# Softcap attention with soft mixture-of-experts slots on one core: weight requests spaced by bytes, the third group's queries requested at the start, engine order recomputed

## The chip, the cores and the metric

The kernel runs on one core of a Trainium2 chip. The metric is the time of one execution on the device, in microseconds (us). The profile is of one execution; its engines are PE (matrix products), ACT (activation functions), DVE (elementwise work), POOL (elementwise work, and the requests of one kind of DMA) and SP (the requests of the other kind).

## The reference

Attention over 8 batches, 12 heads, 448 tokens and 64 features, with a tanh cap on the scores, then a soft mixture of experts with 8 experts of 4 slots each over the 3584 x 768 result:

```python
scores = cap * np.tanh(q @ k.T / sqrt(64) / cap)            # cap = 30, per batch and head
attn = exp(scores - max) / sum                              # softmax over the keys
x = (attn @ v) -> (3584, 768)
logits = x @ phi                                            # phi: (768, 32)
d = softmax(logits, over tokens); slot_input = d.T @ x      # 32 slots
slot_out[e] = relu(slot_input[e] @ w1[e]) @ w2[e]           # w1: (8, 768, 1024), w2: (8, 1024, 768)
out = softmax(logits, over slots) @ slot_out                # (3584, 768) float32
```

## The kernel before

**The work.** Attention runs over 24 groups Q = 0..23; a group is four heads of one batch, so three groups make a batch. The scores of a group are 14 tiles of 128 keys x 448 queries, taken in six chunks of 3, 2, 2, 2, 3 and 2 tiles. For each group:

- `SC` (PE, L515 and L518) makes a chunk of scores in one of two PSUM areas; `TH` (ACT, L528) applies tanh to it and so frees the area. Chunks 0 to 3 (nine tiles) go to the tile `exa`, chunks 4 and 5 (five tiles) to `exd`.
- `EX` (ACT, L536) takes the exponential of the nine tiles of `exa` in one instruction. The five tiles of `exd` are done on DVE instead: four `PH` steps (L543), each making one term of an approximation. There are two `term` buffers, so the third term waits until PE has read the first.
- `PV` (PE, L553) multiplies with the values: parts a0, a1 and d read `exa`, parts c0 to c3 read the four terms. `NR` (DVE, L586 and L587) divides by the sums and writes `xq`.
- `TX` and `CX` (PE L598, DVE L602) transpose `xq`; at the end of a batch `LG` (PE, L622) makes the logits, `EE` (ACT, L632) their exponential, and `ER`, `ET`, `CE`, `SS`, `CS` add the batch to the slot sums.

**The loads.** Queries of a group are requested by POOL (`L q`, L402, cast to bf16 under way, two buffers `qb`) and transposed on PE (`T q`, L485, tile `qps`), then copied by DVE (`C q`, L494). Keys (`LK`, L407, two buffers `kraw`) and values (`LV`, L417, two buffers `vraw`) are requested by SP as float32; `KC` (DVE, L411) casts the keys, and `VC` (POOL, L422) and `VS` (DVE, L425) cast and scale the values. A buffer's next request waits for the work that read it: the queries of group Q wait for `T q` of group Q - 2.

**The weights.** Beside attention POOL requests 56 weight parts (`W`): first 24 parts of w1 of 512 KB each (`w1b`, L338), then 27 parts of w2 of 384 KB that are cast into DRAM (`w2d`, L342) and 5 that stay on chip (`w2b`). These too are cast under way. After attention SP reads the 27 parts back (`w2t`, L867).

**The order.** Every engine works through its own list in order. The lists come from a planner, the class `Plan`: each step gets a due time from its place in the group plus a number of the table `DUE`, a time it may be held for from `HOLD`, and a cost from `COST`; `order()` places steps greedily on a model of the engines. Nothing of this runs on the chip: only the order is left. `load("q", 1)` is emitted ahead of the list. A weight part's due time on POOL is

```python
for k in range(self.parts):
    t = 3000 + k * (NQ * T - T) / self.parts
    op(("W", k), "POOL", C["issue"], (), t, after=t)
```

that is, the 56 parts at equal distances. On the chip a `W` waits for nothing but its turn in POOL's list.

**After attention** come the last group's logits, the slot sums, the first layer (`hp`, L888), the second (`so_ps`, L921) and the output products (L959, L1009), whose results SP stores.

Of the kernel before, what the change touches and what calls it, by code (L numbers as in the profile page):

```python
# [14 lines left out]
ACT = mybir.ActivationFunctionType  # L15
# [10 lines left out]
W = DH + 1  # L26
# [20 lines left out]
TERMS = ((-2.18104, 1.0), (-1.928978, 1.0), (-1.674805, 0.6953125), (-1.419015, 0.6953125))  # L47
PH = len(TERMS)

DUE = {"C0k": 81, "C0q": -150665, "CAk": -64995, "CAq": 68196, "CE": 14263, "CS": 66229, "CW": -188046, "CX":  # L50
# [7 lines left out]
HOLD = {"C0k": 463, "C0q": 1272, "CAk": 739, "CAq": 1395, "CE": 1500, "CW": 856, "Ck": 66, "ER": 1352, "ET": 416,  # L58
# [4 lines left out]
COST = dict(quad=9000, lat=200, dma=7000, form=90, sc=100, scm=200, act=0.833, act0=70, ts=0.265, ts0=70,  # L63
            pvf=31, turn=460, kturn=420, xturn=450, copy=610, norm=830, vcast=1060, vscale=340, kcast=650, kdiag=300,
            issue=800, load=1400, part1=2740, part2=2530, same=300, page=6000)


class Plan:
# [11 lines left out]
    def build(self):  # L80
        C, NQ, NQB = COST, self.NQ, self.NQB
        T = float(C["quad"])
        op = self.op
# [22 lines left out]
        for Q in range(NQ):  # L106
            b, t0, lastq = Q // NQB, Q * T, Q == NQ - 1
            for s in range(nc):
                t = t0 + first[s] * T / NQT
                prev = divmod(Q * nc + s - len(BANKS), nc)  # L110
                tiles = range(first[s], first[s] + CHUNKS[s])
                deps = [("TH",) + prev]
                if Q:
                    deps += [("C", "k", Q), ("C", "q", Q)]
                elif any(TILES[x][0] for x in tiles):
                    deps += [("C0", "k"), ("C0", "q")]
                m = sum(TILES[x][1] is None for x in tiles)
# [24 lines left out]
            te = t0 + .8 * T  # L142
            vs = [("VC", Q), ("VS", Q)]
            op(("PV", Q, "a0"), "PE", 24 * C["pvf"], [("EX", Q, 0)] + vs, te, take=True, mm=24)
            op(("PV", Q, "a1"), "PE", 8 * C["pvf"], [("PV", Q, "a0")], te + 1, mm=8)
            op(("NR", Q, 0), "DVE", C["norm"], [("PV", Q, "a1"), ("SS", (Q - 4) // NQB, 1)], te + 1000,
               give=("PV", Q, "a0"))
            td = t0 + T + 1200
            op(("PV", Q, "d"), "PE", (8 + 4 * (NA - 8)) * C["pvf"], [("EX", Q, 0)] + vs, td - 10, take=True, mm=8 + 4 * (NA - 8))
            for i in range(PH):  # L150
                op(("PV", Q, f"c{i}"), "PE", 4 * nd * C["pvf"],
                   [("PH", Q, i), ("PV", Q, f"c{i - 1}" if i else "d")], td + 1100 * i, mm=4 * nd)
            if ne:
                op(("PV", Q, "e"), "PE", 4 * C["pvf"] * ne, [("EX", Q, 1), ("PV", Q, "c0")], td + 2500, mm=4 * ne)
            op(("NR", Q, 1), "DVE", C["norm"], [("PV", Q, "e"), ("PV", Q, f"c{PH - 1}"), ("SS", (Q - 4) // NQB, 1)],
               td + 5000, give=("PV", Q, "d"))
            if not lastq:
                op(("TX", Q), "PE", C["xturn"], [("NR", Q, 0), ("NR", Q, 1)], t0 + T + 8000, take=True, mm=7)
                op(("CX", Q), "DVE", C["copy"], [("TX", Q), ("LG", (Q - 3) // NQB, 1)], t0 + T + 8700,
                   give=("TX", Q))  # L160
            if Q % NQB == NQB - 1 and not lastq:
                tb = t0 + T + 9500
                op(("LG", b, 0), "PE", 4 * C["scm"], [("CX", Q - 1), ("CX", Q - 2), ("PB",)], tb, take=True, mm=4)
                op(("LG", b, 1), "PE", 2 * C["scm"], [("LG", b, 0), ("CX", Q)], tb + 100, mm=2)
                op(("EE", b), "ACT", 500, [("LG", b, 1), ("ER", b - 1), ("ET", b - 1)], tb + 1300, give=("LG", b, 0))
                op(("ER", b), "POOL", 600, [("EE", b)], tb + 1600, port=True)
                op(("ET", b), "PE", 320, [("EE", b)], tb + 2000, take=True, mm=5)
                op(("CE", b), "DVE", 450, [("ET", b), ("SS", b - 1, 1)], tb + 2300, give=("ET", b))
                op(("SS", b, 0), "PE", 450, [("CE", b)], tb + 3000, take=True, mm=18)
                op(("SS", b, 1), "PE", 250, [("SS", b, 0)], tb + 3100, mm=3)  # L170
                op(("CS", b), "DVE", 400, [("SS", b, 1)], tb + 4500, give=("SS", b, 0))
                if b % 2:
                    op(("ES", b), "PE", 130, [("ER", b), ("ER", b - 1)], tb + 9000, take=True, mm=7)
                    op(("CW", b), "DVE", 200, [("ES", b)], tb + 10000, give=("ES", b))
        op(("PB",), "POOL", 600, (), 20000, after=20000, port=True)
        for k in range(self.parts):
            t = 3000 + k * (NQ * T - T) / self.parts
            op(("W", k), "POOL", C["issue"], (), t, after=t)
            op(("XW", k), "DMA", C["part1"] if k < 24 else C["part2"], [("W", k)], t)
        for o in self.ops.values():  # L180
            o["deps"] = [d for d in o["deps"] if d in self.ops]

# [75 lines left out]
def kernel(  # L258
# [473 lines left out]
    load_k(1)  # L732
    load_v(0)
    load("q", 1)
    pool.dma_start(out=phi4[:, :, 0, :], in_=moe_phi.rearrange("(jt ji) s -> ji jt s", ji=P))
    t = wts.tile([P, 2, 2, NT, DH], BF16, name="casts", tag="w1", bufs=E)
    casts = {(nm, n): t[:, x, n, :, :] for x, nm in enumerate("kq") for n in range(2)}
# [24 lines left out]
        pool.memset(t[HP:P, :, 3, :], 0.0)  # L762
        pool.memset(t[0:HP, :, 4, :], 0.0)

    done = {("L", "q", 1), ("LK", 1), ("LV", 0)}
    for name in order:
        if name[0] in EMIT and name not in done:
            EMIT[name[0]](*name[1:])
# [211 lines left out]
    done = 0  # L980
# [77 lines left out]
```

## Time and profile before

| | |
|---|---|
| median of 3 runs | 297.1 us (296.71 to 299.22) |
| the profiled execution | 298.26 us, of which 296.5 us is the span of the profile and 1.76 us lies around it |
| busy, share of the span | PE 253.4 us (85%), ACT 243.5 (82%), DVE 223.4 (75%), POOL 95.7 (32%) |
| DMA | 75.28 MB, mean 254 GB/s |
| attention on ACT | first tanh at 10.49 us, last at 245.89 us |

A row of the timeline has the start in us, the time in us, the engine, the line, the operation with tiles written <- read, the count of instructions merged, and in brackets the idle time before it and what ended that. A row of DMA issues has the KB of one request and the median us from issue to landing. In the chain of waits each piece has its start, its length and what it was.

### The profile page before, as it was taken

Reading aid. Unit: us, or ns where it says so; the run is one execution under the profiler, and the core shown is the slowest. Engines: PE = TensorE matmul, PEld = TensorE weight load, DVE = VectorE, ACT = ScalarE, POOL = GpSimd, SP = SyncE. Lnnn points to the kernel's source line nnn. Section 1 sums busy time; section 2 is a strip of 40 time slices with the busy share of each in tenths; the row PEclk is TensorE's granted clock in tenths of the full one; section 3 lists DMA queues with packets and bytes.
Section 4 is the critical chain, followed back from the end, with each engine's and each line's share of the span. In section 5 each row is a group of like instructions: output and inputs, shape, how many; then the busy total and the mean of one; then the engine's idle time right before and its main releaser. Section 6 shows DMA issues by size and latency. Waiting matters only on the chain.

```text
span 296.5 us, 10753 instructions
## 1 busy us (share of the span) xinstructions
PE 253.4 (85%) x4674; PEld 176.1 (59%) x4674; DVE 223.4 (75%) x452; ACT 243.5 (82%) x214; POOL 95.7 (32%) x143
## 2 busy tenths in 40 slices
PE   4859979999999949999899999999999988998710
PEld 4337656667676636766677666767667667543300
DVE  2438979888988955989789999897899866246730
ACT  1778998999999993999999999999999994236720
POOL 3553533516260604443335172635061200300000
PEclk9999999999999997999999999999999999999975
DMA  8999999999999999999999999999999698969997
GB/s 146 254 227 220 249 245 246 257 236 246 234 256 242 241 247 245 227 236 240 263 213 185 239 258 225 232 252 251 227 183 259 181 391 227 355 263 335 408 411 306
DMA packets 59070, 75.28 MB, mean 254 GB/s; under 512 B 4880, under 2 KB 48016, under 8 KB 59024
## 3 DMA queue, kind: packets, MB, share of 16 engines
q0 software_dynamic: 30464, 30.50, 61.6%
q1 hardware_dynamic: 28400, 43.89, 46.5%
q8 instruction: 36, 0.59, 0.7%
q10 hardware_dynamic: 160, 0.23, 0.3%
q14 instruction: 10, 0.08, 0.1%
HBM read 94.08 MB, written 21.63 MB: 390 GB/s over the span
## 4 chain that ended last, share of the span: by engine, by line
ACT 29%; DMA 27%; PE 20%; DVE 9%; issue 7%; POOL 2%; SPq 1%; DVEq 0%; ACTq 0%; POOLq 0%
ACT exa L536 14%; DMA vraw<-in_v_dram 12%; DMA qb<-in_q_dram 11%; ACT exd L528 8%; PE pv L553 6%; ACT exa L528 6%; PE sc L518 3%; DVE term L543 3%; DMA out_dram<-ob 2%; PE so_ps L921 2%; PE hp L888 2%; DMA raw<-in_q_dram 2%; PE lps L622 1%; DVE vw L425 1%; DVE ob L1016 1%
## 5 line engine op out<-in xcount | busy, mean ns | idle before, releaser
L528 ACT ACTIVATE exa<-sc 128x1344 f16<-128x1344 f32 (+1 forms) x96 | 92.7, 1027 | 12.0 <-PE sc L518 8.9
L536 ACT ACTIVATE exa<-exa 128x4032 bf16<-128x4032 f16 x24 | 85.6, 3565 | 0.0
L543 DVE TENSOR_SCALAR term<-exd 128x2240 uint16<-128x2240 f16 (+1 forms) x72 | 64.8, 922 | 9.9 <-PE pv L553 7.3
L518 PE MATMUL sc<-qT,kT 64*128 64x448 bf16 x288 | 57.4, 372 | 1.8 <-ACT exa L528 0.3
L553 PEld LDWEIGHTS <-term 128*128 128x128 bf16 x1428 | 48.6, 97 | 14.8 <-DVE term L543 7.7
L528 ACT ACTIVATE exd<-sc 128x1344 f16<-128x1344 f32 (+1 forms) x48 | 53.0, 1104 | 1.0 <-PE sc L518 0.8
L553 PE MATMUL pv<-vb,exa 128*128 128x65 bf16 x1056 | 43.5, 196 | 3.5 <-ACT exa L536 3.0
L553 PEld LDWEIGHTS <-exa 128*128 128x128 bf16 x1056 | 37.4, 99 | 13.6 <-issue 5.7
L402 POOL DMA_DIRECT2D qb<-in_q_dram x23 | 16.9, 735 | 85.9 <-PE qps L485 81.6
L553 PE MATMUL pv<-vb,term 128*128 128x65 bf16 x952 | 37.5, 194 | 1.7 <-DVE term L543 1.7
L422 POOL CAST vb<-vraw 128x1024 bf16<-128x1024 f32 x24 | 26.6, 1110 | 30.9 <-DMA vraw<-in_v_dram 13.3
L587 DVE TENSOR_TENSOR xq<-pv,rec 128x448 bf16<-128x448 f32 (+2 forms) x49 | 30.1, 615 | 1.7
L518 PEld LDWEIGHTS <-kT 64*128 64x128 bf16 x288 | 15.5, 93 | 18.2 <-issue 12.3
L494 DVE COPY qT<-qps 128x896 bf16<-128x896 bf16 x23 | 14.2, 617 | 12.7 <-PE qps L485 12.6
L485 PE MATMUL qps<-ident,qb 128*64 128x128 bf16 x322 | 14.3, 232 | 8.6 <-DMA qb<-in_q_dram 8.6
L543 DVE TENSOR_SCALAR exd<-exd 128x2240 uint16<-128x2240 f16 (+1 forms) x24 | 20.4, 848 | 0.8
L342 POOL DMA_DIRECT2D w2d<-in_moe_w_dram x27 | 20.2, 770 | 0.0
L553 PE MATMUL pv<-vw,term 128*128 128x65 bf16 x476 | 18.7, 193 | 0.1
L553 PE MATMUL pv<-vw,exd 128*128 128x65 bf16 x476 | 18.6, 193 | 0.0
L485 PEld LDWEIGHTS <-qb 128*64 128x64 bf16 x322 | 10.4, 115 | 13.3 <-DMA qb<-in_q_dram 9.4
L515 PE MATMUL sc<-qT,km 128*128 128x448 bf16 x48 | 17.9, 374 | 0.3 <-ACT exa L528 0.2
L338 POOL DMA_DIRECT2D w1b<-in_moe_w_dram x24 | 17.3, 722 | 0.0
(133 smaller groups left out, 306.5 us busy)
## 6 DMA issues: line engine op xcount, KB each, us to landing
w1b<-in_moe_w_dram POOLq DMA_DIRECT2D x24, 512.0 KB, 13.5
w2d<-in_moe_w_dram POOLq DMA_DIRECT2D x27, 384.0 KB, 12.4
w2t<-w2d SPq DMA_DIRECT2D x27, 384.0 KB, 6.0
kraw<-in_k_dram SPq DMA_DIRECT2D x23, 448.0 KB, 9.2
out_dram<-ob SPq DMA_DIRECT2D x9, 768.0 KB, 7.2
vraw<-in_v_dram SPq DMA_DIRECT2D x48, 128.0 KB, 7.4
qb<-in_q_dram POOLq DMA_DIRECT2D x23, 224.0 KB, 9.7
vraw<-in_v_dram SPq DMA_DIRECT2D x48, 96.0 KB, 7.2
```

What stands on the lines that cost most here:

```text
L338: pool.dma_start(out=w1b[e][:, js, :], in_=w1r[:, e, js, :])
L342: pool.dma_start(out=dst, in_=bass.AP(tensor=src.tensor, offset=src.offset + half * HD, ap=[[D, P], [F * D, 4], [1, HD]]))
L402: pool.dma_start(out=t, in_=bass.AP(tensor=srcs[nm].tensor, offset=quad_at(Q), ap=[[NT * DH, P], [2 * S * DH, 2], [1, NT * DH]]))
L422: pool.tensor_copy(vb[Q % 2][:, :, :, 0:DH], vraw[Q % 2])
L485: pe.transpose(ps[h * HP:h * HP + HP, :, x, :], src[:, h, c * DH:(c + 1) * DH], ident)
L515: pe.matmul(dst, km[Q % 2][:, n, :], qT, start=True, stop=True)
L518: pe.matmul(dst, kT[r, 2 * t:2 * t + 2, :], qT[r], start=True, stop=True)
L528: act.activation(quad_ex(Q, u0, u0 + w).bitcast(F16), ring(Q, s)[:, 0:w, 0:S], ACT.Tanh, scale=qk_scale / cap)
L536: act.activation(t, t.bitcast(F16), ACT.Exp, scale=cap)
L543: dve.tensor_scalar(rows(term_home(Q, i))[:, 0:nd, 0:S].bitcast(U16), quad_ex(Q, NA, NA + nd).bitcast(F16), octaves * 128, base[i], ALU.mu ...
L553: pe.matmul(dst[:, 2 * g + h if g < NF else 2 * g, :], buf[:, q0:q0 + P], vt[:, 3 + h if a is None else 5 * h + t, :], start=begin, stop=e ...
L587: dve.tensor_tensor(xq[Q][:, s0:s1, n, :], ps[:, s0:s1, 0:DH], rec.to_broadcast([P, s1 - s0, DH]), op=ALU.mult)
```

## The change

Three things change. The queries of group 2 are requested at the start, next to those of group 1, and so ahead of `phi`. The due times of the weight parts are spaced 4 to 3 for the parts of w1 and w2, as their bytes are, and run to a little later. The tables `DUE`, `HOLD` and part of `COST` are replaced, so that the lists of all engines are computed anew. No instruction is added or taken away on any engine.

```diff
@@ tables (DUE and HOLD get new values throughout)
-DUE = {"C0k": 81, "C0q": -150665, "CAk": -64995, "CAq": 68196, "CE": 14263, "CS": 66229, "CW": -188046, "CX":
...
+DUE = {"C0k": -48926, "C0q": -137122, "CAk": 6246, "CAq": 83143, "CE": -88580, "CS": 94191, "CW": -308673, "CX":
...
-COST = dict(quad=9000, lat=200, dma=7000, form=90, sc=100, scm=200, act=0.833, act0=70, ts=0.265, ts0=70,
+COST = dict(quad=9250, lat=200, dma=6000, form=90, sc=100, scm=200, act=0.833, act0=70, ts=0.265, ts0=70,
             pvf=31, turn=460, kturn=420, xturn=450, copy=610, norm=830, vcast=1060, vscale=340, kcast=650, kdiag=300,
-            issue=800, load=1400, part1=2740, part2=2530, same=300, page=6000)
+            issue=800, load=1400, part1=3200, part2=2450, same=300, page=6000)
@@ Plan.build
+        big = 24
+        total = 4 * big + 3 * (self.parts - big)
         for k in range(self.parts):
-            t = 3000 + k * (NQ * T - T) / self.parts
+            t = 3000 + (4 * min(k, big) + 3 * max(k - big, 0)) * (NQ - 0.4) * T / total
             op(("W", k), "POOL", C["issue"], (), t, after=t)
-            op(("XW", k), "DMA", C["part1"] if k < 24 else C["part2"], [("W", k)], t)
+            op(("XW", k), "DMA", C["part1"] if k < big else C["part2"], [("W", k)], t)
@@ the kernel
     load("q", 1)
+    load("q", 2)
     pool.dma_start(out=phi4[:, :, 0, :], in_=moe_phi.rearrange("(jt ji) s -> ji jt s", ji=P))
...
-    done = {("L", "q", 1), ("LK", 1), ("LV", 0)}
+    done = {("L", "q", 1), ("L", "q", 2), ("LK", 1), ("LV", 0)}
```

The lists are where it shows. Three places follow, each before and after; a line stands three lower in the changed kernel, from L735 on four lower.

POOL in the first two groups, behind its memsets (`qb` is a request of queries, `w1b` one of a weight part, `vb` the cast of a group's values). Before:

```order
L402 DMA qb<-in_q_dram 128x2x448
L338 DMA w1b_87<-in_moe_w_dram 128x2x1024 x2
L402 DMA qb<-in_q_dram 128x2x448
L338 DMA w1b_87<-in_moe_w_dram 128x2x1024
L422 CAST vb_173<-vraw_171 128x16x64
L402 DMA qb<-in_q_dram 128x2x448
```

and now:

```order
L341 DMA w1b_87<-in_moe_w_dram 128x2x1024 x2
L405 DMA qb<-in_q_dram 128x2x448
L425 CAST vb_173<-vraw_171 128x16x64
L405 DMA qb<-in_q_dram 128x2x448
L341 DMA w1b_87<-in_moe_w_dram 128x2x1024
```

The first request of the old rows, the queries of group 2, is gone from here: it now stands ahead of the memsets, directly behind that of group 1. A weight part less stands ahead of the first cast of values.

POOL around the queries of groups 11 and 12. Before (the first `qb` is group 11's, the second group 12's):

```order
L338 DMA w1b_1802<-in_moe_w_dram 128x2x1024
L338 DMA w1b_2069<-in_moe_w_dram 128x2x1024
L402 DMA qb<-in_q_dram 128x2x448
L338 DMA w1b_2069<-in_moe_w_dram 128x2x1024
L422 CAST vb_174<-vraw_172 128x16x64
L402 DMA qb<-in_q_dram 128x2x448
```

and now, the same two requests:

```order
L425 CAST vb_173<-vraw_171 128x16x64
L405 DMA qb<-in_q_dram 128x2x448
L341 DMA w1b_92<-in_moe_w_dram 128x2x1024 x2
L425 CAST vb_174<-vraw_172 128x16x64
L405 DMA qb<-in_q_dram 128x2x448
```

Now each group has its request of queries directly behind the cast of values and ahead of its weight parts, and group 11's comes six weight parts earlier in the count (16 parts stand ahead of it where 22 did). On PE the turns of queries moved likewise: one per group, behind the second chunk of scores, where before they came in threes, the turn of group 11 directly behind the first chunk of group 10.

ACT in group 1 (`exa` <- `sc` is tanh of chunks 0 to 3, `exd` <- `sc` of chunks 4 and 5, `exa` <- `exa` the exponential). Before:

```order
L528 ACTIVATE exa_163<-sc_193 128x3x448
L528 ACTIVATE exa_163<-sc_194 128x2x448
L528 ACTIVATE exa_163<-sc_193 128x2x448
L528 ACTIVATE exa_163<-sc_194 128x2x448
L528 ACTIVATE exd_165<-sc_193 128x3x448
L536 ACTIVATE exa_163<-exa_163 128x9x448
L528 ACTIVATE exd_165<-sc_194 128x2x448
```

and now:

```order
L531 ACTIVATE exa_163<-sc_193 128x3x448
L531 ACTIVATE exa_163<-sc_194 128x2x448
L531 ACTIVATE exa_163<-sc_193 128x2x448
L531 ACTIVATE exa_163<-sc_194 128x2x448
L531 ACTIVATE exd_165<-sc_193 128x3x448
L531 ACTIVATE exd_165<-sc_194 128x2x448
L539 ACTIVATE exa_163<-exa_163 128x9x448
```

In all 24 groups the exponential moved behind the last tanh, so that both chunks of `exd` are ready before it starts and both score areas are free while it runs. On PE the first two chunks of the next group now stand together, and the products of the third and fourth term behind them, that is during the next exponential.

More of the change, by code (lines that the diff above doesn't have):

```diff
@@ L48 @@
 PH = len(TERMS)
-DUE = {"C0k": 81, "C0q": -150665, "CAk": -64995, "CAq": 68196, "CE": 14263, "CS": 66229, "CW": -188046, "CX":
[7 rows of a table removed]
-HOLD = {"C0k": 463, "C0q": 1272, "CAk": 739, "CAq": 1395, "CE": 1500, "CW": 856, "Ck": 66, "ER": 1352, "ET": 416,
[4 rows of a table removed]
-COST = dict(quad=9000, lat=200, dma=7000, form=90, sc=100, scm=200, act=0.833, act0=70, ts=0.265, ts0=70,
+DUE = {"C0k": -48926, "C0q": -137122, "CAk": 6246, "CAq": 83143, "CE": -88580, "CS": 94191, "CW": -308673, "CX":
[7 rows of a table added]
+HOLD = {"C0k": 275, "C0q": 1102, "CAk": 990, "CE": 253, "CS": 996, "CW": 787, "CX": 485, "Cq": 818, "EE": 1500,
[4 rows of a table added]
+COST = dict(quad=9250, lat=200, dma=6000, form=90, sc=100, scm=200, act=0.833, act0=70, ts=0.265, ts0=70,
             pvf=31, turn=460, kturn=420, xturn=450, copy=610, norm=830, vcast=1060, vscale=340, kcast=650, kdiag=300,
-            issue=800, load=1400, part1=2740, part2=2530, same=300, page=6000)
+            issue=800, load=1400, part1=3200, part2=2450, same=300, page=6000)
 class Plan:
@@ L164, in build @@
                 op(("LG", b, 1), "PE", 2 * C["scm"], [("LG", b, 0), ("CX", Q)], tb + 100, mm=2)
-                op(("EE", b), "ACT", 500, [("LG", b, 1), ("ER", b - 1), ("ET", b - 1)], tb + 1300, give=("LG", b, 0))
+                op(("EE", b), "ACT", 550, [("LG", b, 1), ("ER", b - 1), ("ET", b - 1)], tb + 1300, give=("LG", b, 0))
                 op(("ER", b), "POOL", 600, [("EE", b)], tb + 1600, port=True)
                 op(("ET", b), "PE", 320, [("EE", b)], tb + 2000, take=True, mm=5)
-                op(("CE", b), "DVE", 450, [("ET", b), ("SS", b - 1, 1)], tb + 2300, give=("ET", b))
+                op(("CE", b), "DVE", 550, [("ET", b), ("SS", b - 1, 1)], tb + 2300, give=("ET", b))
                 op(("SS", b, 0), "PE", 450, [("CE", b)], tb + 3000, take=True, mm=18)
```

22 rows, old and new, of tables (DUE, HOLD) are left out of this document.

## The prediction

> **What bounds the kernel now.** I read the page first, then ACT's timeline, then the waits, then the chain behind each long one, and last the DMA issues by stage. From the table of stretches:
>
> ```profile
> core 0: us, PE busy (x) PEld busy (x) DVE busy (x) ACT busy (x) POOL busy (x), PEclk, DMA share, GB/s
> 107.00:117.00 10.00, 5.57 (x69) 3.80 (x68) 4.45 (x8) 4.64 (x5) 2.54 (x3) 0.83 1.14 247
> 160.00:205.00 45.00, 43.99 (x846) 31.27 (x843) 40.87 (x79) 44.89 (x39) 19.47 (x25) 1.00 1.21 238
> ```
>
> From 160 to 205 us ACT is busy for 44.89 of 45 us: there attention runs at ACT's pace. From 107 to 117 us all engines stand, while DMA still moves 247 GB/s. So the kernel is bound by ACT where nothing is late, and by loads where something is. ACT's pace, from its timeline:
>
> ```profile
> 10.49 2.91 ACT L528 ACTIVATE exa<-sc 128x1344 f16<-128x1344 f32 x3 [0.35 <-PE sc L515]
> 22.08 2.10 ACT L528 ACTIVATE exa<-sc 128x1344 f16<-128x1344 f32 x2 [2.02 <-PE sc L515]
> 45.86 0.92 ACT L528 ACTIVATE exa<-sc 128x896 f16<-128x896 f32 x1 [1.39 <-PE sc L518]
> 74.73 0.92 ACT L528 ACTIVATE exa<-sc 128x896 f16<-128x896 f32 x1 [0.54 <-PE sc L518]
> 115.94 0.92 ACT L528 ACTIVATE exa<-sc 128x896 f16<-128x896 f32 x1 [5.36 <-PE sc L518]
> 144.56 0.92 ACT L528 ACTIVATE exa<-sc 128x896 f16<-128x896 f32 x1 [0.31 <-PE sc L518]
> 148.13 1.29 ACT L528 ACTIVATE exd<-sc 128x1344 f16<-128x1344 f32 x1 [0.30 <-PE sc L518]
> 162.75 3.88 ACT L528 ACTIVATE exa<-sc 128x1344 f16<-128x1344 f32 x4
> 171.95 2.11 ACT L528 ACTIVATE exa<-sc 128x1344 f16<-128x1344 f32 x2
> 199.89 2.11 ACT L528 ACTIVATE exa<-sc 128x1344 f16<-128x1344 f32 x2
> 209.52 3.86 ACT L528 ACTIVATE exa<-sc 128x1344 f16<-128x1344 f32 x4
> 245.89 0.92 ACT L528 ACTIVATE exd<-sc 128x896 f16<-128x896 f32 x1
> 246.84 0.58 ACT L536 ACTIVATE exd<-exd 128x448 bf16<-128x448 f16 x1
> ```
>
> An undisturbed group takes 171.95 - 162.75 = 9.20 us, one with a batch's exponential 209.52 - 199.89 = 9.63, 0.43 more, in seven groups. Without a stall the 24 groups need 24 x 9.20 + 7 x 0.43 = 223.8 us; they took 245.89 + 0.92 - 10.49 = 236.3. The difference, 12.5 us, is the most that a better order of attention could give. The waits by releaser (total, times, longest) have most of it in one row, on PE's scores:
>
> ```profile
> ACT exa L528 <- PE sc L518: 8.9, 7, 5.4
> ```
>
> PE was late with scores because it works in order and stood at something else. Rows of PE and DVE where that shows:
>
> ```profile
> 20.11 0.96 PE L485 MATMUL qps<-ident,qb 128*64 128x128 bf16 x14 [3.13 <-DMA qb<-in_q_dram]
> 42.45 0.43 DVE L425 TENSOR_SCALAR vw<-vraw 128x512 bf16<-128x512 f32 x1 [1.31 <-DMA vraw<-in_v_dram]
> 111.45 0.78 PE L485 MATMUL qps<-ident,qb 128*64 128x128 bf16 x14 [4.43 <-DMA qb<-in_q_dram]
> ```
>
> and pieces of the chain of waits (start, length, what):
>
> ```profile
> 13.70 6.36 DMA qb<-in_q_dram
> 96.20 15.20 DMA qb<-in_q_dram
> 129.90 11.71 DMA qb<-in_q_dram
> ```
>
> So 2.02 us are the queries of group 2, asked for at 13.70 only; 1.39 are the values of group 3, for which DVE stood until 42.45 with the terms behind them, and 0.54 likewise those of group 6; 5.36 are the queries of group 11, which took 15.20 us; 0.61 (0.31 + 0.30) are those of group 14, which took 11.71 us. Together 9.9 us of stalls end at a load. The other 2.6 are short waits that the order itself makes.
>
> **The change, part by part.** It adds and removes no instruction, so each term is a wait.
>
> Group 2's queries at the start: the 2.02 us go, since a request at the start has until about 20 us. It puts one request and 224 KB beside the first loads, ahead of phi. Those are what the start waits for. ACT's first work, and DMA up to 14 us:
>
> ```profile
> 6.51 1.28 ACT L454 ACT_TABLE_LOAD   x1 [6.51 <-DMA raw<-in_q_dram]
> ```
>
> ```profile
> DMA packets 3071, 2.78 MB, mean 198 GB/s; under 512 B 1044, under 2 KB 3071, under 8 KB 3071
> ```
>
> Bounds: nothing, if the first raw loads have landed at 6.5 us before the second request moves data; or 224 KB at the 198 GB/s of the first 14 us, 1.1 us. The request stands behind group 1's on the same queue, so I take 0.3. What else it delays (keys and values of the next groups) is needed behind the first exponential only, some 10 us later.
>
> The turns of queries, one per group: before, the request for group 11 could only go out once the turn of group 9 had run, late in group 8, at 96.20, and PE wanted the data early in group 10, at 111.45 - 4.43 = 107.0, that is 10.8 us later. Now the turns are 9.2 us apart and a request waits for the turn two groups earlier, so it has 18.4 us less the cast and the issue ahead of it, some 16. What a load takes, by stage (14 to 60, 60 to 112 and 160 to 205 us):
>
> ```profile
> w1b<-in_moe_w_dram POOLq DMA_DIRECT2D x14, 512.0 KB, 12.7
> ...
> w1b<-in_moe_w_dram POOLq DMA_DIRECT2D x11, 512.0 KB, 16.7
> qb<-in_q_dram POOLq DMA_DIRECT2D x5, 224.0 KB, 14.2
> ...
> w2d<-in_moe_w_dram POOLq DMA_DIRECT2D x13, 384.0 KB, 10.9
> qb<-in_q_dram POOLq DMA_DIRECT2D x5, 224.0 KB, 8.4
> ```
>
> Even 14.2 us fits into 16, so the 5.36 and 0.61 go.
>
> Weight parts: in POOL's list 16 parts now stand ahead of group 11's queries, not 22, so some 10 parts fall in the 46 us from 14 to 60 where there were 14. There and up to 112 us loads were slow (12.7 and 16.7 us against 10.9 later), and the values came late. With a quarter of the weights gone from that stage the 1.39 and 0.54 go. They come back later: 33 parts, all but one of 384 KB, stand in the last 12 groups, 2.75 a group. From 160 to 205 us, 13 parts in 45 us are 2.66 per 9.2 us, at 238 GB/s and with ACT at 44.89 of 45. So the late half of the change asks 3% more than a stretch that ran without a stall. Bounds 0 to 1.4 us (the one late load of values, again); I take 0.3.
>
> The exponential behind the last tanh, in every group: this moves all that PE and DVE do. While ACT is in the exponential PE now makes the next two chunks, which it may since both areas are free, then the products of terms 3 and 4, a turn and the transposes; behind it come part a0 and chunk 2. That chunk waits for the first tanh (1.29 us for three tiles) and has about 0.8 us to be made in. The new wait to look at: terms 3 and 4 wait for PE's product of term 1, which now stands behind the last chunk; then come product 4, the division, the transpose, and only then a0 and chunk 2. What is queued behind the transpose on PE is thus ACT's next tanh but one. The nearest rows:
>
> ```profile
> L543 DVE TENSOR_SCALAR term<-exd 128x2240 uint16<-128x2240 f16 x15 | 13.7, 934 | 1.3 <-PE pv L553 1.0
> L543 DVE TENSOR_SCALAR exd<-exd 128x2240 uint16<-128x2240 f16 x5 | 4.3, 858 | 0.2
> L587 DVE TENSOR_TENSOR xq<-pv,rec 128x448 bf16<-128x448 f32 x9 | 5.6, 624 | 0.3
> L518 PE MATMUL sc<-qT,kT 64*128 64x448 bf16 x60 | 11.7, 357 | 0.3
> L485 PE MATMUL qps<-ident,qb 128*64 128x128 bf16 x70 | 2.9, 222 | 0.0
> L422 POOL CAST vb<-vraw 128x1024 bf16<-128x1024 f32 x5 | 5.7, 1136 | 4.1 <-PE pv L553 3.2 <-issue 1.0
> ```
>
> The chain from product 1: two terms 0.93 + 0.86, product 4 about 0.7 (20 of the 60 that take 2.15 us further below), division 0.62: 3.1 us. PE's own work from there to the transposes: products 2 to 4 (2.1), two chunks of five tiles (5 x 11.7 / 60 = 1.0), a turn (14 x 2.9 / 70 = 0.6): 3.7. The chain is the shorter by 0.6, so PE need not wait. Bounds: 0 a group, as from 160 to 205; or one short wait as the 0.30 at 148.13 in each, 22 x 0.30 = 6.6. Nearest to the first, since DVE is busy for only 40.87 of 45 us: I take 0.05 a group, 1.1 us.
>
> The end: the last exponential now ends 0.6 us before ACT's last instruction, where it ended 1.5 us before it (245.89 against 247.42). All 112 products of the last group stand behind it on PE, about 3.8 us by the next rows (60 in 2.15, the last 32 in 1.33); before, the last ended at about 250.2.
>
> ```profile
> 246.06 2.15 PE pv L553 x60
> 248.23 0.64 DVE term L543
> 248.92 1.33 PE pv L553 x32
> ```
>
> That is 247.4 - 0.6 + 0.1 + 3.8 = 250.7 on the old clock, 0.5 later; with the last weight parts asked for nearer the end I take 0.7. Bounds -0.3 (the 0.64 us of a late term no longer in the way) to 2.
>
> Sum: -9.9 + 0.3 + 0.3 + 1.1 + 0.7 = -7.5 us. The profiled span becomes 296.5 - 7.5 = 289.0, its execution 290.8; the median of the runs lay 1.16 below the profiled execution (297.1 against 298.26), which gives 289.6.
>
> **The rivals.** First, all stalls go, the short ones too: 12.5 less 0.7 at the end, 11.8, gives 285.3. For it: with both score areas free during the exponential PE can run ahead by two chunks. Against: part of the short waits lie in the first two groups, which the change does not speed up.
>
> Second, the loads stay late: weights moved to the second half slow it as they did the first. One 5.36 us stall again leaves 2.1 of the gain, 295.0. For it: DMA share is 1.21 at 160 to 205 us, higher than the 1.14 at 107 to 117. Against: with that share loads took 8 to 11 us, and the tolerance is now 16.
>
> Third, POOL's casts of values hold DVE up. The cast (1.14 us) now becomes free to start behind product 4 in every group, when DVE has the division, the copies and the next terms. If each cast stops DVE for its whole length, DVE's idle time, (45 - 40.87) / 45 x 9.2 = 0.85 us a group, covers all but 0.29, and 22 x 0.29 = 6.4 in place of the 1.1 gives 294.9. Against: the mean of a term, 0.93 against 0.86 for the one in `exd`, says that few casts hit a term in the old order.
>
> That rule stands in the Trainium skill, "SBUF — State Buffer", section "Who interferes with whom": DVE in its two-port modes and GpSimd share a pair of ports, and whoever comes second stands still for the whole instruction. The means of the terms agree with a lock that is seldom met and do not show its full length.
>
> Fourth, slower than before: the chain from product 1 to the transpose is longer than PE's work in the same stretch. Each group then pays the excess. It decides from (9.9 - 1.3) / 22 = 0.4 us a group on, when gains of 9.9 less the other 1.3 are eaten; at 0.55 a group the time is 297.1 - 8.6 + 12.1 = 300.6. For it: PE, DVE and ACT are all over 90% busy from 160 to 205 us. Against: DVE has 0.85 us a group free, and the chain 0.6 of margin.
>
> That the change does not move what is late falls: the list of POOL shows group 11's request moved.
>
> **How the numbers follow.** The forecast 0.56, the first rival 0.15, the second 0.09 and the third 0.07 (each near 295, half of it within 1%), the fourth 0.13, of which 0.03 within 1% and 0.10 above. A measurement of this kernel tells about 1% from no change: below 294.1 is faster, above 300.1 slower. So faster 0.79 (0.56 + 0.15 + 0.08), the same 0.11, slower 0.10. The likeliest case spans 286.5 to 292.5; the range takes in the first rival at 285.3 and the second and third at 295.0 and 294.9, with half a microsecond to one beyond: 284.8 to 296.0.
>
> **What would show it.** Right: no query load ends a wait of PE over 1 us; ACT starts group 1 at about 20.1 us; groups in the middle take 9.2 to 9.3 us from the start; the last tanh at about 238 us. Wrong: waits of ACT on PE's scores of some tenths in every group, with PE at the transposes waiting for DVE's division (the fourth rival), casts of values beside long terms (the third), or PE or DVE waiting for `vraw`, `kraw` or `qb` past 120 us (the second). If the first group starts over 0.5 us later than 10.49, the early request is dearer than I took it.

## The result: 0.7% slower, the loads' stalls gone and a wait in two groups of three in their place

| | before | after |
|---|---|---|
| median | 298.23 us (296.09 to 300.26) | 300.43 us (298.50 to 301.75) |
| ratio after/before | | 1.0073 (95%: 1.0049 to 1.0097) |
| profiled span | 296.5 us | 298.0 us |

The forecast was 289.6 us from a before of 297.1 (2.5% less), in a range up to 296.0, so the measured time lies outside it. The slowdown is real but under the 1% that the prediction called no change. The table of stretches of the changed kernel, to be held against the two stretches of before that the prediction shows (line numbers are 3 to 4 higher in the changed kernel):

```profile
core 0: us, PE busy (x) PEld busy (x) DVE busy (x) ACT busy (x) POOL busy (x), PEclk, DMA share, GB/s
60.00:112.00 52.00, 49.13 (x935) 34.81 (x935) 46.23 (x89) 49.66 (x43) 17.97 (x22) 1.00 1.08 227
160.00:205.00 45.00, 42.62 (x819) 30.27 (x818) 40.33 (x74) 43.50 (x37) 17.66 (x22) 1.00 1.21 229
```

There is no longer a stretch in which all engines stand. But from 160 to 205 us, where ACT was busy for 44.89 of 45 us, it is now busy for 43.50. The timeline of ACT shows the same wait, ahead of the tanh of chunk 2, in two groups of three:

```profile
147.49 2.17 ACT L531 ACTIVATE exa<-sc 128x1344 f16<-128x1344 f32 x2
150.30 1.88 ACT L531 ACTIVATE exa<-sc 128x896 f16<-128x896 f32 x2 [0.65 <-PE sc L521]
...
154.09 3.56 ACT L539 ACTIVATE exa<-exa 128x4032 bf16<-128x4032 f16 x1
157.54 2.10 ACT L531 ACTIVATE exa<-sc 128x1344 f16<-128x1344 f32 x2
160.16 1.88 ACT L531 ACTIVATE exa<-sc 128x896 f16<-128x896 f32 x2 [0.52 <-PE sc L521]
...
163.95 3.57 ACT L539 ACTIVATE exa<-exa 128x4032 bf16<-128x4032 f16 x1
...
173.45 3.63 ACT L539 ACTIVATE exa<-exa 128x4032 bf16<-128x4032 f16 x1
```

From one exponential of nine tiles to the next, the groups with the wait take 163.95 - 154.09 = 9.86 us and, two groups later, 183.55 - 173.45 = 10.10, not 9.20. The group between them takes 173.45 - 163.95 = 9.50 us: it has a batch's exponential and no wait, and such groups took 9.50 to 9.63 before, where nothing was late. The view of waits (total, times, longest) has PE at the transposes when ACT waits:

```profile
ACT exa L531 <- PE sc L521: 9.2, 16, 0.9
PEld L601 <- DVE xq L590: 8.4, 15, 1.1
PE xps L601 <- DVE xq L590: 6.2, 15, 1.0
```

Before, the 8.9 us of ACT's waits on L518 were seven waits, and four of them, 7.6 us, ended at a load. Now 9.2 us are sixteen waits of 0.2 to 0.9 us behind PE's own chain. The sums are alike by chance. Group 1 starts at 20.20 us (20.1 was forecast), the first tanh at 9.98.

**Why the chain is late.** The chain of waits in one group of the changed kernel, from the third term to the transposes (start, length, what):

```profile
153.61 0.87 DVE term L546
154.48 0.02 issue
154.50 0.04 DVE exd L546
154.54 1.45 issue
155.99 0.83 DVE term L546
156.83 0.53 DVE kcast L414
...
157.39 0.21 DVE rec L589
157.60 0.02 issue
157.62 0.63 DVE xq L590
158.26 0.05 issue
158.31 0.56 PE xps L601 x7
```

The piece to look at is "1.45 issue": DVE waits for nothing that the profile records, in the middle of the fourth term. The timeline of both engines at that place says what runs beside it:

```profile
153.61 0.86 DVE L546 TENSOR_SCALAR term<-exd 128x2240 uint16<-128x2240 f16 x1
154.31 1.05 POOL L425 CAST vb<-vraw 128x1024 bf16<-128x1024 f32 x1 [3.86 <-PE pv L556]
154.50 1.56 DVE L546 TENSOR_SCALAR exd<-exd 128x2240 uint16<-128x2240 f16 x1
```

POOL's cast of the values starts 0.2 us ahead of the fourth term, and that term takes 1.56 us in place of 0.86. In the group with the batch's exponential (163.95) the cast starts 0.04 us behind the fourth term: that term takes 0.86 us there, and it is the term behind it that takes longer, 1.46. By groups of instructions, from 60 to 230 us, after and then before:

```profile
L546 DVE TENSOR_SCALAR term<-exd 128x2240 uint16<-128x2240 f16 x52 | 48.5, 933 | 0.6
L546 DVE TENSOR_SCALAR exd<-exd 128x2240 uint16<-128x2240 f16 x17 | 22.6, 1327 | 0.6
L425 POOL CAST vb<-vraw 128x1024 bf16<-128x1024 f32 x17 | 20.0, 1175 | 57.1 <-PE pv L556 45.1 <-issue 10.6 <-DMA vraw<-in_v_dram 1.4
```

```profile
L543 DVE TENSOR_SCALAR exd<-exd 128x2240 uint16<-128x2240 f16 x17 | 14.6, 858 | 0.6
```

The fourth term went from 858 to 1327 ns. The cast is mostly released by a product of PE (45.1 of its 57.1 us of idle time): its buffer `vb` was last read by product c1 two groups back, since c2 and c3 read `vw`. So it becomes free behind product 2, not behind product 4 as the prediction had it, and that is when DVE goes through terms 3 and 4.

### The profile page after: what moved, and what is told of

Same layout as the page of the kernel before. It is cut to its first block, busy times and chain, and to the rows that moved or that the text cites. A ratio compares the mean times of both kernels' runs of the same rounds, so it can differ in the third digit from the quotient of the medians.

```text
span 298.0 us, 10770 instructions
## 1 busy us (share of the span) xinstructions
PE 258.1 (87%) x4674; PEld 177.9 (60%) x4674; DVE 231.0 (78%) x452; ACT 245.0 (82%) x214; POOL 96.9 (33%) x143
## 4 chain that ended last, share of the span: by engine, by line
PE 50%; DVE 24%; issue 8%; DMA 7%; ACT 3%; SPq 2%; DVEq 0%; ACTq 0%
PE pv L556 21%; PE sc L521 11%; DVE term L546 9%; DVE xq L590 4%; DMA kraw<-in_k_dram 4%; PE xps L601 3%; DVE kcast L414 3%; PE lps L625 3%; PE kps L484 2%; PE sc L518 2%; DMA out_dram<-ob 2%; PE so_ps L925 2%; PE hp L892 2%; DMA vraw<-in_v_dram 2%; SPq L441 1%
## 5 line engine op out<-in xcount | busy, mean ns | idle before, releaser
L531 ACT ACTIVATE exa<-sc 128x1344 f16<-128x1344 f32 (+1 forms) x96 | 94.1, 1026 | 10.8 <-PE sc L521 9.2
L546 DVE TENSOR_SCALAR term<-exd 128x2240 uint16<-128x2240 f16 (+1 forms) x72 | 67.0, 932 | 9.0 <-PE pv L556 4.7
L556 PEld LDWEIGHTS <-term 128*128 128x128 bf16 x1428 | 48.7, 98 | 12.4 <-issue 11.1
L531 ACT ACTIVATE exd<-sc 128x1344 f16<-128x1344 f32 (+1 forms) x48 | 50.8, 1116 | 0.6 <-PE sc L521 0.5
L425 POOL CAST vb<-vraw 128x1024 bf16<-128x1024 f32 x24 | 28.0, 1168 | 63.9 <-PE pv L556 51.9
L556 PE MATMUL pv<-vb,exa 128*128 128x65 bf16 x1056 | 45.3, 197 | 1.3 <-ACT exa L539 0.8
L556 PEld LDWEIGHTS <-exa 128*128 128x128 bf16 x1056 | 38.6, 99 | 12.2 <-issue 7.0
L546 DVE TENSOR_SCALAR exd<-exd 128x2240 uint16<-128x2240 f16 (+1 forms) x24 | 30.7, 1278 | 0.8
L494 DVE COPY kT<-kps 128x768 bf16<-128x768 bf16 x23 | 12.7, 553 | 12.7 <-PE kps L484 12.0
L556 PEld LDWEIGHTS <-exd 128*128 128x128 bf16 x480 | 16.3, 97 | 5.5 <-DVE exd L546 5.4
L601 PE MATMUL xps<-ident,xq 128*128 128x128 bf16 x161 | 12.9, 220 | 6.2 <-DVE xq L590 6.2
L518 PE MATMUL sc<-qT,km 128*128 128x448 bf16 x48 | 17.7, 369 | 0.1
(133 smaller groups left out, 298.7 us busy)
```

The source lines that it names most:

```text
L425: pool.tensor_copy(vb[Q % 2][:, :, :, 0:DH], vraw[Q % 2])
L518: pe.matmul(dst, km[Q % 2][:, n, :], qT, start=True, stop=True)
L531: act.activation(quad_ex(Q, u0, u0 + w).bitcast(F16), ring(Q, s)[:, 0:w, 0:S], ACT.Tanh, scale=qk_scale / cap)
L546: dve.tensor_scalar(rows(term_home(Q, i))[:, 0:nd, 0:S].bitcast(U16), quad_ex(Q, NA, NA + nd).bitcast(F16), octaves * 128, base[i], ALU.mu ...
L556: pe.matmul(dst[:, 2 * g + h if g < NF else 2 * g, :], buf[:, q0:q0 + P], vt[:, 3 + h if a is None else 5 * h + t, :], start=begin, stop=e ...
L601: pe.transpose(ps[:, h, g * P:min(g * P + P, S)], x_cols(Q, h, g).rearrange("p n d -> p (n d)"), ident)
```

## The experiments

Most of the runs change the emission list right behind `order, bank_of = plan.order()`; what else a run changes is in its edit. The kernel before took 298.5 to 298.7 us beside them.

**1. The cast alone moved.**

```diff
+    for Q in range(3, NQ - 3):
+        move(("VC", Q), ("L", "q", Q + 3))     # the cast directly behind the request for queries
```

> The changed kernel, with POOL's cast of the values of groups 3 to 20 moved behind the request for the queries three groups on, which waits for a turn behind product 4; nothing else is moved. Theory A (the cast starts together with the fourth term and DVE stands still for it): the fourth term falls from 1.28 us to about 0.86, the middle groups from 9.85 to 9.3 to 9.45 us, the kernel from 300.4 to 290 to 293 us, and ACT's waits of 0.4 to 0.9 us on scores go or fall under 0.3. Theory B (the chain product 1, terms 3 and 4, product 4, division, transposes is too long in this order whatever POOL does): groups stay at 9.75 to 9.85 us and the time within 1.5 us of 300.

Measured: 294.59 us, ratio to before 0.9835 (0.9754 to 0.9917); 5.8 us less than the change, though above theory A's 290 to 293. The view of groups, 60 to 230 us, and the engines in one group with a batch's exponential:

```profile
L554 DVE TENSOR_SCALAR term<-exd 128x2240 uint16<-128x2240 f16 x55 | 54.5, 993 | 0.7
L554 DVE TENSOR_SCALAR exd<-exd 128x2240 uint16<-128x2240 f16 x18 | 17.1, 950 | 0.6
```

```profile
158.91 3.57 ACT L547 ACTIVATE exa<-exa 128x4032 bf16<-128x4032 f16 x1
...
160.89 0.21 DVE L597 RECIPROCAL rec<-pv 128x7 f32<-128x7 f32 x1 [0.54 <-PE pv L564]
161.13 0.62 DVE L598 TENSOR_TENSOR xq<-pv,rec 128x448 bf16<-128x448 f32 x1
...
162.20 1.97 DVE L554 TENSOR_SCALAR term<-exd 128x2240 uint16<-128x2240 f16 x1
162.40 1.06 POOL L433 CAST vb<-vraw 128x1024 bf16<-128x1024 f32 x1
...
164.10 0.60 DVE L613 COPY xT<-xps 128x896 bf16<-128x896 bf16 x1
...
164.75 0.54 PE L633 MATMUL lps<-xT,phi 128*128 128x448 bf16 x2 [0.68 <-DVE xT L613]
...
168.97 3.58 ACT L547 ACTIVATE exa<-exa 128x4032 bf16<-128x4032 f16 x1
```

The cast still stops DVE in every third group, and here for its whole length: 1.97 is 0.86 + 1.06 within 0.05. The Trainium skill ("SBUF — State Buffer", "Who interferes with whom") gives that length: the engine that comes second stands still for the whole instruction of the other. Its order does not show in these rows, in which the stopped term starts 0.20 us ahead of the cast. In the other two groups of three the cast falls mostly beside DVE's copies, and the timeline shows no term over 1.10 us there.

Theory A holds in kind: with the cast away from the third and fourth term, the groups without a batch's exponential take 9.12 to 9.26 us in place of 9.82 to 10.13, and ACT has no wait in them. But its size is missed, and the trace shows where. In every third group the stopped term stands ahead of the copy of the transposes (`xT`), PE's logits wait 0.68 us for that copy, and the group takes 168.97 - 158.91 = 10.06 us. In the change the same kind of group takes 9.50. There a term is stopped too (1.46 us), and ACT does not wait. So it is not DVE's lost time that costs, but what waits for the stopped term.

**2. The cast made twice, at its place in the change.**

```diff
         pool.tensor_copy(vb[Q % 2][:, :, :, 0:DH], vraw[Q % 2])
+        if 3 <= Q < NQ - 3:
+            pool.tensor_copy(vb[Q % 2][:, :, :, 0:DH], vraw[Q % 2])
```

> The changed kernel, with each cast of values of groups 3 to 20 made twice, one behind the other, at the same place. Theory A: the second cast (1.05 us) stops the term behind the fourth one, which stands ahead of the division, so the groups grow by 0.3 to 1.0 us more, to 10.1 to 10.9 us, and the kernel to 306 to 318 us. Theory B: POOL has some 5 us a group free, so nothing changes: 300 us, within 1.5.

Measured: 309.63 us, 1.0327 (1.0237 to 1.0417), 9.2 us over the change, 0.51 for each of 18 casts. With run 1, theory B is out.

**3. Early queries of group 2 alone, in the kernel before.**

```diff
     load("q", 1)
+    load("q", 2)
-    done = {("L", "q", 1), ("LK", 1), ("LV", 0)}
+    done = {("L", "q", 1), ("L", "q", 2), ("LK", 1), ("LV", 0)}
```

> The kernel before, with the queries of group 2 requested at the start with those of group 1, and nothing else. If the parts add up as the prediction has them, the 2.02 us stall at 22 us goes and the later ones stay: 296.0 to 296.7 us where the kernel before takes 298.2, first tanh as before within 0.3 us. Rival: ACT's next wait takes the place of it, or the later loads slip with it, and the time stays within 0.5 us of the kernel before.

Measured: 298.75 us, 1.0002 (0.9972 to 1.0031): worth nothing alone. The stall at 22 us is gone, but ACT at group 11, the turn of the queries, and the chain of waits read:

```profile
116.72 0.92 ACT L528 ACTIVATE exa<-sc 128x896 f16<-128x896 f32 x1 [8.11 <-PE sc L518]
```

```profile
111.56 0.96 PE L485 MATMUL qps<-ident,qb 128*64 128x128 bf16 x14 [6.60 <-DMA qb<-in_q_dram]
```

```profile
94.26 17.26 DMA qb<-in_q_dram
```

The queries were asked for 1.94 us sooner than before (94.26 against 96.20) and took 2.06 us longer (17.26 against 15.20): they land at 111.52 and 111.40 us. Asking sooner did not bring them sooner; that what stood ahead of them in the queues decided it is the likely reason, which run 4 bears out. The stall at this load swallowed what was won ahead of it.

**4 and 5. The spacing alone, and the order alone.** Both take the first change (early queries) and set how many weight parts stand ahead of each group's queries:

```diff
+    ahead = [...]      # run 4, in the old order: as the change (16 ahead of group 11)
+                       # run 5, in the new order: as before (22 ahead of group 11)
+    parts = [x for x in order if x[0] == "W"]
+    order = [x for x in order if x[0] != "W"]
+    ...
```

Half of a group's parts go behind the last request for queries, half ahead of the next. So the place of a part between two requests is not quite that of the change (run 4) or of the kernel before (run 5); only the counts are.

> The kernel before, with the queries of group 2 requested at the start and with as many weight parts ahead of each group's queries as the changed kernel has; the order of all other work is the old one. Theory A says that the spacing of the parts alone takes the loads' stalls away (5.36, 1.39, 0.61, 0.54 us) and that only the new order of the engines costs something: 288 to 291 us, groups of 9.2 to 9.3 us, no stall over 1 us. Rival C: the late queries of group 11 came from the old order (their request stood behind a late turn), so 3 to 6 us of stalls stay and the time is 292 to 297 us.

> The changed kernel (new order of the engines, early queries of group 2), with as many weight parts ahead of each group's queries as the kernel before has. If the spacing removed the late loads (theory A): the request for group 11 finds 22 parts ahead of it again, ACT stalls by 2 to 8 us at loads between 60 and 120 us, and the time is 302 to 307 us against 300.4 of the change. If the new order with its earlier requests removed them (theory C): no load ends a wait of ACT over 1 us, and 300 to 301.5 us.

Measured, run 4: 290.37 us, 0.9717 (0.9663 to 0.9771). Run 5: 306.47 us, 1.0260 (1.0209 to 1.0311). With these the change comes apart (all four with early queries):

| median, us | parts as before | parts spaced by bytes |
|---|---|---|
| old order | 298.75 | 290.37 |
| new order | 306.47 | 300.43 |

The spacing is worth 8.4 us in the old order and 6.0 in the new one; the new order costs 7.7 and 10.1. In run 4 no stall is left in the stretch where all stood, and in run 5 it is back:

```profile
60.00:112.00 52.00, 50.74 (x1009) 36.76 (x1005) 46.15 (x95) 51.84 (x44) 18.97 (x24) 1.00 1.07 227
160.00:205.00 45.00, 43.49 (x875) 31.70 (x872) 39.89 (x82) 44.88 (x39) 18.27 (x23) 1.00 1.24 240
```

```profile
118.62 0.92 ACT L543 ACTIVATE exa<-sc 128x896 f16<-128x896 f32 x1 [6.74 <-PE sc L533]
```

So the spacing, not the new order, brings the loads in time (theory C is out). One wait of 1.19 us, behind the values of an early group, is left in run 4, at 42.21 us. Run 4 also has a new wait behind attention:

```profile
ACT obh L976 <- PE op L972: 7.4, 6, 5.4
```

Ten weight parts are left for its last groups; the last five took 21.8 us to land by their median (10.5 before), and ACT waits 5.4 us at once for the second layer, 7.4 in all (2.1 and 3.9 before).

**6. The spacing without the early queries, in the old order** (run 4 without its two lines of `load("q", 2)` and `done`).

> The kernel before with the weight parts spaced as in the change and nothing else: no early queries of group 2. The early queries alone were worth nothing (298.75 against 298.53 us) since ACT then stood 8.1 us, not 5.4, for group 11's queries, which landed at the same 111.4 us of the clock. Theory A: with nothing late behind them their 2.02 us show, so this takes 291.9 to 293.0 us, against 290.4 with them. Rival: they are worth nothing here either, 290.0 to 290.9 us.

Measured: 292.91 us, 0.9815 (0.9759 to 0.9871). With the later parts spaced the early queries are worth 292.91 - 290.37 = 2.5 us, as theory A had it, near the 2.02 of the sum. (The intervals of the two ratios still overlap a little.) The trace does not show the 2.02 us come back, though: ACT waits 0.64 us at the start of group 1 and 4.22 us at 46.15, behind values that took 14.40 us, where run 4 waits 1.19. It is of the slowest of the four executions, 295.19 us. So the size agrees, and the way in which it comes is open.

**7. A denser spacing, in the old order.** As run 4, with 52 parts in place of 46 by group 23.

> The kernel before with early queries of group 2 and spaced weight parts, with the last parts asked for sooner: 52 of the 56 stand ahead of group 23's queries, not 46, with the gain in groups 15 to 22. With 46 the last five parts took 21.8 us to land (10.5 before) and the second layer's weights were waited for, 5.4 us on ACT behind the attention. Theory A: those 5.4 us go but for about one, 285 to 287.5 us, and the middle groups stay at 9.2. Rival: the denser requests make loads late in groups 15 to 22 and the time stays at 289 to 292 us.

Measured: 299.20 us, 0.9995 (0.9960 to 1.0031). My theory fell, and the rival's range of 289 to 292 is passed too: the 5.4 us at the end went (2.1 left), but 3.2 parts a group, not 2.6, are more than the DMA carried beside the other loads. PE waits for queries again, and ACT is busy for 38.15 of 45 us:

```profile
PE qps L497 <- DMA qb<-in_q_dram: 6.9, 5, 3.0
```

```profile
160.00:205.00 45.00, 39.65 (x731) 29.07 (x726) 36.45 (x70) 38.15 (x33) 19.19 (x25) 0.92 1.25 236
```

It moved 236 GB/s there, no more than run 4 with 240. My second rival is real, and it starts between 2.6 and 3.2 parts a group.

**8. The end.** Run 1, and the last group's order on ACT and DVE as before:

```diff
+    order.remove(("EX", NQ - 1, 0))
+    order.insert(order.index(("TH", NQ - 1, 5)), ("EX", NQ - 1, 0))
+    move(("PH", NQ - 1, 0), ("CX", NQ - 2))
+    move(("PH", NQ - 1, 1), ("PH", NQ - 1, 0))
```

> The changed kernel with the casts of groups 3 to 20 moved behind the request for queries (as in the run that took 294.6 us), and with the last group's order on ACT as before: its first exponential ahead of its last tanh, and the last group's terms 1 and 2 behind the copy of the transposes on DVE. Theory: PE can start the last products about 1 us earlier against ACT's end, and its clock stays up (0.54 at 246 to 249 us in the change, 1.00 before): 1 to 2 us less than 294.6, so 292.5 to 293.6 us. Rival: PE is only shifted, since DVE's late terms end the products: 294.0 to 295.0 us.

Measured: 292.85 us, 0.9804 (0.9757 to 0.9851). Against run 1 that is 1.7 us less, but the intervals overlap; the trace is clearer. The end of attention on PE, in the change and here:

```profile
246.37 2.60 PE L556 MATMUL pv<-vb,exa 128*128 128x65 bf16 x44 [0.77 <-ACT exa L539]
248.79 1.52 PE L556 MATMUL pv<-vb,term 128*128 128x65 bf16 x32
...
251.19 0.67 PE L556 MATMUL pv<-vw,exd 128*128 128x65 bf16 x16
```

```profile
238.84 1.54 PE L569 MATMUL pv<-vb,exa 128*128 128x65 bf16 x44
...
242.35 0.67 PE L569 MATMUL pv<-vw,exd 128*128 128x65 bf16 x16
```

ACT ended at 246.79 in the change and at 240.20 here, so PE's last product came 251.86 - 246.79 = 5.07 us behind ACT in the change, 4.73 in run 1, 2.82 here, and 2.83 in the kernel before. Here the granted clock stays at 1.00 from 236 to 244 us.

**9 and 10. An even spacing, in the old order.** As run 4, with 50 (run 9) and 48 (run 10) parts by group 23.

> The kernel before with early queries of group 2 and weight parts spaced evenly in bytes from group 8 on: about 2.5 parts (mostly 512 KB) ahead of each group's queries up to group 13, then 2.7 parts of 384 KB a group, 50 of 56 by group 23. The run with 2.6 parts a group late and ten left for the end took 290.4 us, with 5.4 us waited for the last weights; 3.2 parts a group took 299.2, with queries late by up to 4.5 us. If about 2.7 parts a group is still what the DMA carries beside the other loads at 240 GB/s: 286 to 289 us. Rival: the carrying limit lies below that, loads are late in groups 10 to 23 again, 291 to 297 us.

> As the run before, but milder: about 2.3 parts a group up to group 13, then 2.7, with 48 of 56 by group 23 and eight for the end. If the limit lies between 2.7 and 3.2 parts: 287 to 289.5 us, the wait for the last weights 2 to 4 us in place of 5.4, groups of 9.2. Rival (limit lower): 290 to 294 us.

Measured: 292.86 us, 0.9798 (0.9762 to 0.9834), and 290.30 us, 0.9719 (0.9682 to 0.9755). Run 9 lies within the rival's range, with stalls of 2.14 and 3.59 us on ACT at groups 12 and 22 in its trace. Run 10 has none over 0.6 us, waits 2.4 us for the last weights in place of 5.4, and is yet no faster than run 4 by its median. That misses my 287 to 289.5 and lies in the rival's 290 to 294, but no late load shows for it; the trace is of its fastest execution, 288.1 us. I leave the cause open.

**11. The cast made twice in the old order** (run 4 with the edit of run 2).

> The kernel before with early queries of group 2 and the spacing of the change (290.4 us), with each cast of values of groups 3 to 20 made twice. In the new order a second cast took the time from 300.4 to 309.6 us, 0.51 us for each of 18 casts. Theory A (it is the place that costs: there the cast meets the terms between product 1 and the transposes, which PE and then ACT wait for): in the old order the same second cast meets DVE at the division and copies, or terms that nothing is late for, so under 0.15 us each, 290 to 293 us. Rival (each cast stops DVE, which is over 85% busy, so its time comes back in full or half wherever it stands): 0.3 to 0.5 us each, 296 to 300 us.

Measured: 292.68 us, 0.9795 (0.9717 to 0.9874): 2.3 us more than run 4, 0.13 for each cast, where the new order paid 0.51. In the traces 2.1 us of it stand in the groups from the exponential of group 2 to that of group 4, 56.24 - 34.13 = 22.11 us in place of 53.85 - 33.85 = 20.00. From ACT's timeline, the twelve groups from the exponential of group 5 to that of group 17:

| | us a group | against the row above it |
|---|---|---|
| old order, run 4 | (174.97 - 63.03) / 12 = 9.33 | |
| old order, cast twice, run 11 | (177.87 - 65.42) / 12 = 9.37 | 0.04 |
| new order, cast late, run 1 | (178.22 - 64.68) / 12 = 9.46 | |
| new order, the change | (183.55 - 66.03) / 12 = 9.79 | 0.33 |
| new order, cast twice, run 2 | (192.67 - 69.25) / 12 = 10.29 | 0.50 |

Each row holds 0.14 us for a batch's exponential (0.43 in every third group). Against run 1, one cast at its place in the change costs 0.33 us a group, two cost 0.83. In the old order a second cast costs next to nothing, and it seldom meets a term there: from 60 to 230 us the mean of a `term` is 924 ns in run 11 against 889 in run 4, and that of the fourth term 859 in both.

The 0.13 us by which run 1 stays above run 4 is no toll in every group. Over these twelve groups its four with a batch's exponential take 10.02 to 10.06 us against 9.51 to 9.62, and its other eight 9.12 to 9.26 against 9.18 to 9.29. So what is left is in the groups where the moved cast stops the term ahead of `xT`. Were it gone there too, the new order would take an estimated (9.15 + 9.25 + 9.50) / 3 = 9.30 us a group, with the 9.50 from the change: no more than the old order. No run has the new order without any such stop, so this is not shown.

## Why the prediction was wrong, step by step

**The loads (-9.9): right, with a wrong reading of their sum.** No load ends a wait of ACT in the changed kernel, and the spacing with early queries takes the old order from 298.5 to 290.4, 8.1 us, though 3.5 us of waits for the last weights came new with it (7.4 against 3.9). But the terms do not add one by one: the early queries, priced at 2.02 us, were worth nothing while the stall at group 11 stood behind them (run 3), and 2.5 with the parts spaced (run 6).

**The start (+0.3) and the late half (+0.3): too dear, by little.** The first tanh came at 9.98 us, not later; no load was late. That the late half lies near its limit, as the second rival said, runs 7 and 9 show.

**The exponential behind the last tanh (+0.05 a group): this step failed.** In the twelve groups of the table it measured 9.79 - 9.33 = 0.46 us a group. Over groups 2 to 23 the change took 242.75 - 27.35 = 215.40 us and run 4 230.97 - 24.52 = 206.45: 8.95 us in place of 1.1. I set a chain of 3.1 us against 3.7 of PE's work and found 0.6 of margin. The trace has 158.24 - 153.61 = 4.63 us from the third term to the end of the division. Two things were left out:

- What DVE has queued ahead of the division: the next group's first term (0.83) and the cast of keys (0.53 to 0.60). Product 4 covers only part of it. This alone makes 3.93 us in run 1 (149.28 to 153.21), where the cast is elsewhere. That is over the 3.7, and yet ACT does not wait there.
- POOL's cast beside the fourth term, which makes the 3.93 into 4.63; against run 1 it costs 0.33 us a group. I had it behind product 4, from the planner's dependence on the values, where in the trace the last reader of the buffer (product c1) releases it; and I let DVE's idle time cover it. Idle time elsewhere in the group does not cover a delay inside a chain that PE waits for.

The comparison with 3.7 us was itself the wrong test. What goes with ACT's wait is how long behind the exponential's start PE comes to the transposes, not the length of the chain:

| stretch, by the exponential that starts in it | third term to division, us | transposes behind that start, us | ACT's wait for chunk 2, us |
|---|---|---|---|
| the change, 154.09 | 4.63 | 158.31 - 154.09 = 4.22 | 0.52 |
| the change, 163.95 | 3.93 | 167.10 - 163.95 = 3.15 | none |
| run 1, 149.76 | 3.93 | 153.27 - 149.76 = 3.51 | none |
| run 1, 168.97 | 4.71 | 172.59 - 168.97 = 3.62 | none |

The row quoted against a lock, terms of 0.93 and 0.86 us, only said that in the old order the cast stood elsewhere. It said nothing on the new one, in which POOL comes to the cast early and only product c1 holds it.

**The fourth rival was what happened**, at 300.6 us with 0.55 a group; I gave it 0.13. The third had its cause, with a cover that was not there: they were one case, not two. That 300.6 lies so near the measured 300.43 is in part luck: the excess a group was smaller, and a slow group 1 and a slow end, which the rival had not priced, made up for it.

**The end (+0.7): mis-sized, about 2.2.** Against ACT's end the last product came 5.07 - 2.83 = 2.24 us later; ACT itself ended 247.42 - 246.79 = 0.63 us sooner, so on the clock it came 1.6 later, where 0.5 was forecast. The 112 products took 5.5 us, not 3.8: 44 of them 2.60 in place of 1.54 in run 8, with the granted clock at 0.54 from 246 to 249 us.

**What the new order costs beside run 4**, by the two traces (spans 298.0 and 288.9): attention on ACT, from the first tanh to the end of the last exponential, took 246.79 - 9.98 = 236.8 us against 235.95 - 10.24 = 225.7, that is 11.1 more. From the start of the first exponential of nine tiles to that of the last it is 226.79 us against 215.53, and run 1 takes 221.31. So 226.79 - 221.31 = 5.5 go with the cast at its place (5.8 by the medians; 18 x 0.33 = 5.9 by the table). The other 5.8 are read off the traces of run 1 and run 4, exponential by exponential, and not run apart: 1.7 in group 1 (10.80 us against 9.08; 11.39 in the change), 2.7 in six middle groups with a batch's exponential, and 3.1 in the last three, whose casts run 1 leaves where the change has them, less 1.7 in the others, mostly by an early group (9.15 us against 10.35, with run 4's wait of 1.19). Why group 1 is slower stays open. Behind attention the change is 1.8 shorter (51.2 against 53.0) in spite of its slow end, since run 4 waits for its last weights there (7.4 us of ACT's waits at L976; 3.8 at the same step of the change).

## What to carry to other kernels

Before pricing a reordering, write down the one chain that the bounding engine will wait for, with everything that stands in each engine's list between its links, and ask of each link what runs on the other engines at that moment; average idle time is no cover for it. Look up what really releases an instruction (the last reader of its buffer) rather than the planner's idea of it. Stalls at loads did not add here: try the cures together and one by one.

## What the runs showed of the hardware

- A POOL cast can stop a DVE term for the cast's whole length: 1.97 us for a 0.86 us term beside a 1.06 us cast. A cast that started 0.04 us behind a term of 0.86 took 1.48 us in place of 1.05, that is 0.43 more. In the chain of waits a stopped term shows only as "issue", 1.45 us.
- Queries asked for 1.94 us sooner (run 3) landed 0.12 us later (111.52 against 111.40 us).
- The granted clock at the end of attention, by the table of stretches of the change and then of before:

```profile
243.00:246.00 3.00, 1.55 (x34) 1.13 (x30) 2.48 (x6) 3.00 (x1) 0.00 (x0) 1.00 1.04 402
246.00:249.00 3.00, 2.63 (x48) 2.63 (x49) 0.26 (x1) 0.78 (x2) 0.00 (x0) 0.54 1.04 412
```

```profile
243.00:246.00 3.00, 0.93 (x19) 0.63 (x15) 1.45 (x3) 3.00 (x2) 0.00 (x0) 1.00 1.00 291
246.00:249.00 3.00, 2.83 (x83) 2.67 (x84) 1.90 (x4) 1.39 (x3) 0.00 (x0) 1.00 0.68 247
```

It fell to 0.54 behind three us with PE busy for 1.55, and stayed at 1.00 behind three us with only 0.93. How full the last three us were does not tell it. The Trainium skill ("TensorE: Matmul & The Clock Gate", "Part 1: The HAM clock gate") says that the window in which activity is counted runs free of the kernel; that would fit, and no run here shows it.
